# Decay rows of the first head pair: from a 66-partition sum in place instead of through DRAM, with the first constants, copies and loads reordered

## The chip, the cores and the metric

The kernel runs on one core of one Trainium2 chip. The metric is device microseconds of one launch. The profiler records one execution; its times are in microseconds from the first instruction. Engines are named as in the profile: PE multiplies matrices (PEld loads its weights), DVE, ACT and POOL work element by element, SP issues most transfers.

## What is computed

Three layers in a row. The first, causal attention with a decay from cumulative sums, is the one that the change touches:

```python
B, H, S, D = 4, 8, 576, 64
scores = (1 / np.sqrt(D)) * np.matmul(q, k.transpose(0, 1, 3, 2))
cum = np.cumsum(np.log(np.clip(f, 0.0001, 1.0)), axis=-1)        # f: (B, H, S)
decay = cum[:, :, :, None] - cum[:, :, None, :]
scores = np.where(causal, -1e9, scores + decay)                  # causal: above the diagonal
attn = np.exp(scores - scores.max(-1, keepdims=True))
attn = attn / (attn.sum(-1, keepdims=True) + 1e-9)
x = np.matmul(attn, v)                                           # 2304 tokens of 512
```

Then each token goes through the one of 8 experts that its logits choose (512 to 1024 to 512, ReLU, gated), and through a dense layer 512 to 2048 to 512 with a rational activation. The softmax takes away whatever is constant along a row, so only the term -cum of the key position has to be added to the scores.

## The kernel before, in words

**Pairs.** The 32 heads are worked off as 16 pairs of heads (`pair(p)`), four pairs to a batch element. A pair has its q and k transposed (two 64-row copies each, `rq` and `rk`, loaded at L374) and its v (L382, L383). A head's scores come in 128-row steps `i`, in the order of `steps`: head 0 with i = 2 and 3 first (384 and 512 columns), then the 64-row tails of both heads (288 columns, two halves), and the rest.

**Full precision by splitting.** The score product is made of high and low parts in the fp32r type. `kh` (L411) is the high part of k, `kl` (L416) what is left of it, `qs` (L422, L425) and `q2s` (L430) the same for q. A score tile takes two products: L456 (`kh` with `qs`) and L457 (`kl` with `q2s`), for the tails L467 and L468.

**The decay as two more rows.** Of the tile `kl` (a 64-row half for each head), two rows in the other head's half carry the sum cum/SCALE, split in a high and a low part; `q2s` holds ones there. So the second product adds the decay. `qs`, `q2s` and `kl` have two buffers each, for even and odd pairs, zeroed once by POOL at the start (L232 to L243).

**How the sums are made.** All 32 heads at once on 32 partitions, width 576: load f (L303), clip (L322), logarithm on ACT (L311), running sum (L315), high part on ACT (L329), low part on DVE (L333). Both parts are stored to DRAM as `cum_d` (L338). Every pair, the first included, then loads its four rows from there into `kl` (`load_c`, L388).

**What sets the order.** `Plan` is a list scheduler at build time. Each `plan.op` has a due time (`when`), a length in ns for each engine that may do it, needs, and buffers taken and freed. Among the operations that are ready on an engine it starts the one that is due first. The lengths and the due times (`T_STEP`, `T_TRANS`, `T_MOVE` ...) are constants in the code. Each engine and each DMA queue then does its instructions in the order that came out, so an early operation that moves can reorder all that come later in the attention stage. On PE the first 80 operations are idle matmuls on constants (`idle`, L353), before the first scores.

**Downstream of the scores.** `least` (L479, L491) takes the scores out of PSUM with the mask and the minimum, `weights` (L511, L522) makes the exponentials on ACT, PE transposes them (L598, L578), ACT or DVE copies them (`evac`, L291 and L293), and PE multiplies by v (L621). When the four pairs of a batch element are done, its five row blocks are scaled by DVE into tiles `xr` (L796, three buffers) and stored to `x_d` by POOL's queue (L823). After the last batch the token routing is computed and the expert layer starts.

Of the kernel before, what the change touches and what calls it, by code (L numbers as in the profile page):

```python
# [9 lines left out]
F32 = mybir.dt.float32  # L10
F32R = mybir.dt.float32r
# [4 lines left out]
AF = mybir.ActivationFunctionType  # L16
ALU = mybir.AluOpType
# [4 lines left out]
P = 128  # L22
# [115 lines left out]
def tile_attention_moe_mlp(  # L138
# [72 lines left out]
    oh = ec.tile([P, NE, NCOL], BF16, name="oh")  # L211
    pref = ec.tile([P, NE], F32, name="pref")
    nc.gpsimd.iota(pref, pattern=[[-1, NE]], base=NE, channel_multiplier=0, allow_small_or_imprecise_dtypes=True)

    prefs = ec.tile([P, NI, NE], F32, name="prefs")
    nc.gpsimd.tensor_copy(prefs, pref.unsqueeze(1).to_broadcast([P, NI, NE]))
    nc.gpsimd.memset(prefs[TL:, NQ], 0.0)


    with ExitStack() as actx, ExitStack() as rctx:  # L220
# [7 lines left out]


        qs = [wk.tile([P, 2, S + P], F32R, name=f"qs{i}", bufs=1) for i in range(2)]  # L230
        for t in qs:
            nc.gpsimd.memset(t.bitcast(F32)[:, :, S:], 0.0)  # L232
        half = (slice(0, D), slice(D, P))

# [3 lines left out]
        kls = [ld.tile([P, 2, S], F32R, name=f"kl{i}", bufs=1) for i in range(2)]  # L238
        for t, k in zip(q2s, kls):
            nc.gpsimd.memset(t.bitcast(F32), 0.0)  # L240
            nc.gpsimd.memset(k.bitcast(F32), 0.0)
            for h in range(2):
                nc.gpsimd.memset(t.bitcast(F32)[half[1 - h].start : half[1 - h].start + 2, h, 0:S], 1.0)  # L243

# [3 lines left out]

        mask = wk.tile([P, NQ * P], F32, name="mask", bufs=1)
        mask_t = wk.tile([P, S // 2], F32, name="mask_t", bufs=1)  # L250
        nc.gpsimd.memset(mask, 0.0)
        nc.gpsimd.memset(mask_t, 0.0)
        for t in [mask[:, (NQ - 1) * P :]] + [mask_t[h * TL : (h + 1) * TL, S // 2 - TL :] for h in range(2)]:
            nc.gpsimd.affine_select(
                out=t, in_=t, compare_op=ALU.is_ge, fill=BIG / SCALE, base=0, pattern=[[-1, t.shape[-1]]], channel_multiplier=1
            )

# [22 lines left out]
        def wt(tag, shape=(P, S)):  # L280
            return wk.tile(list(shape), F32, tag=tag, name=tag, bufs=plan.buffers.get(tag, 2))
# [17 lines left out]
        g0 = {}  # L299

        def f_load(e):
            g0["fl"] = wt("t")[:NBH]
            nc.sync.dma_start(out=g0["fl"], in_=f)  # L303

        def f_zero(e):
            g0["zf"] = wt("pr")[:NBH]
            nc.vector.memset(g0["zf"], 0.0)

        def f_log(e):
            g0["lf"] = wt("pr")[:NBH]  # L310
            nc.scalar.activation(g0["lf"], g0["fl"], AF.Ln)  # L311

        def f_scan(e):
            g0["cum"] = wt("t")[:NBH]
            nc.vector.tensor_tensor_scan(  # L315
                out=g0["cum"], data0=g0["lf"], data1=g0["zf"], initial=0.0, op0=ALU.add, op1=ALU.add
            )
# [3 lines left out]
        o_f = plan.op(early, {"SP": 1900}, f_load, takes=["t"])  # L321
        o_c = plan.op(early, {"DVE": 369}, lambda e: nc.vector.tensor_scalar(  # L322
            g0["fl"], g0["fl"], 1.0e-4, 1.0, op0=ALU.max, op1=ALU.min), [o_f])
        o_l = plan.op(early, {"ACT": 573}, f_log, [o_c], takes=["pr"], frees=[("t", o_f)])
        o_cum = plan.op(early, {"DVE": 669}, f_scan, [o_l, o_z], takes=["t"], frees=[("pr", o_z), ("pr", o_l)])

        def f_high(e):
            g0["ch"] = wt("pr")[:NBH].bitcast(F32R)
            nc.scalar.activation(g0["ch"], g0["cum"], AF.Copy, scale=1.0 / SCALE)  # L329

        def f_low(e):
            g0["cl"] = wt("pr")[:NBH].bitcast(F32R)
# [28 lines left out]
        def pair(p):  # L361
# [29 lines left out]
            for h0, h1 in one:  # L391
# [15 lines left out]
            def kh(h):  # L407
                def go(e):
                    if h == 0:
                        d["kh"] = lt("kh", (P, 2, S), F32R)  # L410
                    nc.vector.tensor_copy(d["kh"][:, h], d["rk"][:, h])  # L411
                return go
# [16 lines left out]
            def q2h(h):  # L429
                return lambda e: (nc.vector if e == "DVE" else nc.gpsimd).tensor_scalar(  # L430
                    q2[half[h], h, 0:S], d["rq"][half[h], h], 1.0, 1.0, op0=ALU.mult, op1=ALU.mult
                )
# [108 lines left out]
            for si, step in enumerate(steps):  # L541
# [4 lines left out]
                if i < NQ:  # L546
                    n, m = (i + 1) * P, len(hs)
                    need = [x[h] for h in hs for x in (o_kh, o_kl, o_qh, o_ql, o_q2)] + [l_c, pt_first[0]]
                    o_s = plan.op(w, {"PE": 2 * m * (max(n, 256) / 2.4 + 14)}, scores(hs, i, u), need, takes=["s"] if pt_first[0] else ["s", "pT"])
                    pt_first[0] = pt_first[0] or o_s  # L550
                    o_l_ = plan.op(w + T_LEAST * SPAN, {"DVE": m * (120 + 1.042 * n)}, least(hs, i, u), [o_s], takes=["t"], frees=[("s", o_s)])
                    d["o_exp"].append(None)
                    o_e = first_e = plan.op(w + T_EXP * SPAN, {"ACT": m * (360 + 0.85 * n)}, weights(hs, i, u), [o_l_], takes=["pr"], frees=[("t", o_l_)])
                    d["o_exp"][-1] = o_e
                    all_s.append(o_s)
                else:
                    prev, first_e = None, None
                    for c in (0, hw):
                        o_s = plan.op(w, {"PE": 4 * (hw / 2.4 + 14)}, scores_tail(c, u), o_kh + o_kl + o_qh + o_ql + o_q2 + [l_c, pt_first[0]], takes=["s"])
# [326 lines left out]
        plan.op(SPAN, {"SP": 1300}, load_wl, [st[0]["o_ot"]])  # L886

        with tc.manual_schedule():
            plan.emit()
# [761 lines left out]
```

## Time and profile before

| | us |
|---|---|
| median of 3 runs | 891.31 (890.9 to 892.05) |
| the profiled execution's own time | 889.93 |
| its span, first to last instruction | 888.2 |
| PE busy over the span | 849.3 (96%) |
| DVE busy | 747.9 (84%) |
| ACT busy | 615.6 (69%) |
| POOL busy | 337.5 (38%) |

The attention stage takes the first 204 us or so; the routing, the expert layer and the dense layer follow. PE's busy time counts overlapping matmuls as one stretch and hides how well a stretch is filled, so the stage is read from gaps on PE and from who ended them. The chain of work that ended last, which the page also gives, reaches back only into the expert layer, and says nothing of the first stage.

### The profile page before, as it was taken

Reading aid. Unit: us, or ns where it says so; the run is one execution under the profiler, and the core shown is the slowest. Engines: PE = TensorE matmul, PEld = TensorE weight load, DVE = VectorE, ACT = ScalarE, POOL = GpSimd, SP = SyncE. Lnnn points to the kernel's source line nnn. Section 1 sums busy time; section 2 is a strip of 40 time slices with the busy share of each in tenths; the row PEclk is TensorE's granted clock in tenths of the full one; section 3 lists DMA queues with packets and bytes.
Section 4 is the critical chain, followed back from the end, with each engine's and each line's share of the span. In section 5 each row is a group of like instructions: output and inputs, shape, how many; then the busy total and the mean of one; then the engine's idle time right before and its main releaser. Section 6 shows DMA issues by size and latency. Waiting matters only on the chain. (4 is left out here: it accounts for less than half of the span.)

```text
span 888.2 us, 15292 instructions
## 1 busy us (share of the span) xinstructions
PE 849.3 (96%) x4667; PEld 705.0 (79%) x4667; DVE 747.9 (84%) x1428; ACT 615.6 (69%) x1282; POOL 337.5 (38%) x364
## 2 busy tenths in 40 slices
PE   6999898996999999999999999999999999999997
PEld 6787786764888887888787788899888889988885
DVE  7798999778798878778876999898898878988882
ACT  4889897876465667567545878777676667777772
POOL 7888586502113232223241233343233224324222
PEclk9999999997999999999999999999999999999999
DMA  6776567604866588789564121010000001000001
GB/s 167 167 182 168 154 175 212 199 27 151 298 218 217 177 263 310 226 288 316 195 218 154 48 72 37 0 60 24 13 36 25 12 1 57 16 1 36 1 0 48
DMA packets 49130, 110.32 MB, mean 124 GB/s; under 512 B 8405, under 2 KB 12526, under 8 KB 49038
## 3 DMA queue, kind: packets, MB, share of 16 engines
q1 hardware_dynamic: 36910, 69.90, 26.4%
q0 software_dynamic: 12128, 39.34, 13.3%
q8 instruction: 40, 0.66, 0.3%
q14 instruction: 52, 0.43, 0.2%
HBM read 151.79 MB, written 20.35 MB: 194 GB/s over the span
## 5 line engine op out<-in xcount | busy, mean ns | idle before, releaser
L1519 POOL TENSOR_TENSOR gl<-raw,gh 128x512 fp32r<-128x512 f32 (+1 forms) x71 | 84.2, 1186 | 207.3 <-ACT gh L1517 127.2
L1535 PE MATMUL pa<-wu,gl 128*128 128x512 f32 x256 | 100.6, 393 | 1.1 <-POOL gl L1519 1.1
L1533 PE MATMUL pa<-wu,gh 128*128 128x512 f32 x256 | 101.2, 395 | 0.0
L1534 PE MATMUL pa<-wu,gh 128*128 128x512 f32 x256 | 100.1, 391 | 0.0
L1492 ACT ACTIVATE raw<-ph 128x512 f32<-128x512 f32 (+1 forms) x80 | 44.3, 554 | 78.1 <-PE ph L1484 74.8
L1058 DVE TENSOR_TENSOR wu<-raw,wu 128x1024 fp32r<-128x1024 f32 x64 | 75.2, 1219 | 8.0 <-ACT wu L1056 6.6
L511 ACT ACTIVATE pr<-t,mn 128x384 f32<-128x384 f32 (+3 forms) x128 | 70.7, 557 | 16.0 <-DVE mn L479 15.4
L1505 DVE SCALAR_TENSOR_TENSOR raw<-raw,coef,raw 128x512 f32<-128x512 f32 (+1 forms) x80 | 66.2, 827 | 17.8 <-ACT raw L1501 15.1
L1495 DVE SCALAR_TENSOR_TENSOR raw<-raw,babs 128x512 f32<-128x512 f32 (+1 forms) x80 | 58.3, 729 | 20.9 <-ACT raw L1493 20.2
L1482 PE MATMUL ph<-colAh,wi 128*128 128x512 f32 x192 | 74.9, 390 | 1.0 <-ACTq L1423 0.7
L1484 PE MATMUL ph<-colAh,wi 128*128 128x512 f32 x192 | 74.7, 389 | 0.0
L1483 PE MATMUL ph<-colAl,wi 128*128 128x512 f32 x192 | 74.7, 389 | 0.0
L1056 ACT ACTIVATE wu<-raw 128x1024 fp32r<-128x1024 f32 x64 | 63.8, 1066 | 4.1 <-DMA raw<-in_w_dram 2.2
L479 DVE CUSTOM_DVE_ANT_0 t<-s,mask 128x384 f32<-128x384 f32 (+3 forms) x128 | 57.8, 484 | 6.5 <-PE s L457 3.0
L1506 DVE SCALAR_TENSOR_TENSOR raw<-raw,cbias 128x512 f32<-128x512 f32 (+1 forms) x80 | 57.6, 720 | 2.3
L1500 ACT ACTIVATE raw<-raw,cbias 128x512 f32<-128x512 f32 (+1 forms) x80 | 55.0, 687 | 6.3 <-DVE raw L1495 5.8
L1494 ACT ACTIVATE raw<-ph,neg 128x512 f32<-128x512 f32 (+1 forms) x80 | 59.3, 741 | 0.0
L1535 PEld LDWEIGHTS pa<-wu,gl 128*128 128x128 f32 x256 | 48.0, 188 | 12.7 <-POOL gl L1519 2.4
L1497 DVE SCALAR_TENSOR_TENSOR raw<-raw,coef,ph 128x512 f32<-128x512 f32 (+1 forms) x80 | 55.5, 694 | 2.5
L1533 PEld LDWEIGHTS pa<-wu,gh 128*128 128x128 f32 x256 | 48.1, 188 | 9.5 <-ACT gh L1517 0.7
L1534 PEld LDWEIGHTS pa<-wu,gh 128*128 128x128 f32 x256 | 48.1, 188 | 9.0
L1507 DVE SCALAR_TENSOR_TENSOR raw<-raw,raw 128x512 f32<-128x512 f32 (+1 forms) x80 | 52.4, 655 | 2.4
(263 smaller groups left out, 2391.9 us busy)
## 6 DMA issues: line engine op xcount, KB each, us to landing
raw<-in_w_dram SPq DMA_DIRECT2D x92, 1024.0 KB
rk<-in_kT_dram SPq DMA_DIRECT2D x30, 288.0 KB
rq<-in_qT_dram SPq DMA_DIRECT2D x30, 288.0 KB
d<-in_w_in_dram POOLq DMA_DIRECT2D x16, 512.0 KB
d<-in_w_out_dram POOLq DMA_DIRECT2D x16, 512.0 KB
y_d<-ys SPq DMA_DIRECT2D x22, 256.0 KB
v<-in_v_dram SPq DMA_DIRECT2D x16, 256.0 KB
wo_d<-d POOLq DMA_DIRECT2D x16, 256.0 KB
```

The costliest lines, as they stand in the source:

```text
L511: nc.scalar.activation(u["pr"][:, sl], u["t"][:, sl], AF.Exp, bias=u["mn"][:, m : m + 1], scale=-1.0, accum_out=sm[:, i, 2 * hp + h : 2 * ...
L1056: nc.scalar.activation(w[:, 0], r, AF.Copy)
L1058: nc.vector.tensor_tensor(w[:, 1], r, w[:, 0].bitcast(F32), ALU.subtract)
L1482: nc.tensor.matmul(out_, wh, hi[:, :, c], start=(c == 0), stop=False)
L1483: nc.tensor.matmul(out_, wh, lo[:, :, c], start=False, stop=False)
L1484: nc.tensor.matmul(out_, wl_, hi[:, :, c], start=False, stop=(c == KD - 1))
L1494: nc.scalar.activation(u_, ph, AF.Identity, scale=neg[:, 3:4], bias=neg[:, 2:3])
L1505: nc.vector.scalar_tensor_tensor(u_, u_, coef[:, 0:1], rr, ALU.subtract, ALU.mult)
L1519: low.tensor_tensor(d["gl"], d["u_"], d["gh"].bitcast(F32), ALU.subtract)
L1533: nc.tensor.matmul(a_, gh[:, sl], wh, start=(m == 0), stop=False)
L1534: nc.tensor.matmul(a_, gh[:, sl], wl_, start=False, stop=False)
L1535: nc.tensor.matmul(a_, gl[:, sl], wh, start=False, stop=(m == MF - 1))
```

## The change

- **Sums.** The sum is made over 66 partitions: rows 32 to 63 hold the 32 heads as before, rows 64 and 65 both hold head 0, and rows 0 to 31 all hold head 1 (of which rows 0 and 1 are used). So head 0's rows end up on the partitions where pair 0's `kl` wants them, and so do head 1's. A per-partition factor `sgn` gives on partitions 0 and 64 the high part, on 1 and 65 the low part. `f_rows` writes these pairs of rows straight into `kl` of pair 0, one two-row DVE instruction per head. Pair 0 has no `load_c`.
- **Loads of f.** Three instead of one: two on SP's queue, one on ACT's, ahead of the table load.
- **Stores of the sums.** Still made, for pairs 1 to 15, but due later, and the low part (`f_low`) is due later too; `f_rows(1)` and `f_low` also need a `least` of pair 0 each.
- **First constants.** `kl` of pair 0 is zeroed by DVE, `after` and `onesb` come first on POOL, then what pair 0 needs, then the mask and the identity, then pair 1's buffers, the small tables last.
- **Copies.** For pair 0, `q2s` of both heads and `kh` of head 1 go from DVE to ACT.
- **Coefficients.** The two loads of `coef` move from the start into the plan, after pair 1.

```diff
+    sgn = ec.tile([P, 2], F32, name="sgn")
+    nc.vector.memset(sgn, 1.0 / SCALE)
+    for r in (0, D):
+        nc.vector.memset(sgn[r : r + 1, 0:1], -1.0 / SCALE)
+        nc.vector.memset(sgn[r : r + 1, 1:2], 0.0)
...
+        def blank(i, on):
+            t = q2s[i].bitcast(F32)
+            on.memset(kls[i].bitcast(F32), 0.0)
+            nc.gpsimd.memset(t, 0.0)
...
+        blank(0, nc.vector)
...
         def f_load(e):
-            g0["fl"] = wt("t")[:NBH]
-            nc.sync.dma_start(out=g0["fl"], in_=f)
+            g0["fl"] = wt("t")
+            nc.scalar.dma_start(out=g0["fl"][D:NF], in_=f[0:1, :].to_broadcast([2, S]))
+            nc.sync.dma_start(out=g0["fl"][F0], in_=f)
+            nc.sync.dma_start(out=g0["fl"][0:NBH], in_=f[1:2, :].to_broadcast([NBH, S]))
+            nc.scalar.preload_act_table_set("natural_log_exp_and_others")
...
+        def low_of(rows, to):
+            nc.vector.scalar_tensor_tensor(
+                to, g0["cum"][rows], sgn[rows, 1:2], g0["ch"][rows].bitcast(F32), ALU.mult, ALU.subtract
+            )
+
+        def f_rows(h):
+            r = half[1 - h].start
+            return lambda e: low_of(slice(r, r + 2), kls[0][r : r + 2, h, :])
...
-        o_cl = plan.op(early, {"DVE": 669}, f_low, [o_ch], takes=["pr"], frees=[("t", o_cum)])
+        o_first = [plan.op(early, {"DVE": 669}, f_rows(0), [o_ch], takes=["c"])]
+        o_first.append(plan.op(-1.2 * SPAN, {"DVE": 669}, f_rows(1), [o_ch]))
+        o_cl = plan.op(-1.1 * SPAN, {"DVE": 669}, f_low, [o_ch], takes=["pr"], frees=[("t", o_cum)])
         o_cst = [
-            plan.op(early, {"SP": 650}, f_store(0, "ch"), [o_ch], frees=[("pr", o_ch)]),
-            plan.op(early, {"SP": 650}, f_store(1, "cl"), [o_cl], frees=[("pr", o_cl)]),
+            plan.op(-0.9 * SPAN, {"SP": 650}, f_store(0, "ch"), [o_ch], frees=[("pr", o_ch)]),
+            plan.op(-0.9 * SPAN, {"SP": 650}, f_store(1, "cl"), [o_cl], frees=[("pr", o_cl)]),
         ]
...
-            l_c = plan.op(tl + 0.3 * SPAN, {"SP": 1200}, load_c, o_cst, takes=["c"])
+            l_c = plan.op(tl + 0.3 * SPAN, {"SP": 1200}, load_c, o_cst, takes=["c"]) if p else o_first[0]
...
-                o_kh.append(plan.op(w, {"DVE": 420}, kh(h), [lk[h]] + o_kh[:1], takes=["kh"] if h == 0 else []))
+                o_kh.append(plan.op(w, {"DVE": 420} if p or h == 0 else {"ACT": 620}, kh(h), [lk[h]] + o_kh[:1], takes=["kh"] if h == 0 else []))
...
-                q2e = {"POOL": 1340} if p else {"DVE": 400}
+                q2e = {"POOL": 1340} if p else {"ACT": 620}
...
+                    if p == 0 and si < 2:
+                        (o_first[1], o_cl)[si].needs.append(o_l_)
...
+        plan.op(2 * SPAN, {"SP": 1300}, load_coef, [st[1]["o_ot"]])
```

**Order on SP, at the start.** From the loads of head 1's k of pair 0 (64x576) on; the loads of 64x1152 are those of pair 1. Before:

```order
L374 DMA rk<-in_kT_dram 64x576 x2
L338 DMA cum_d<-pr 32x576
L374 DMA rq<-in_qT_dram 64x576 x2
L902 DMA coef<-in_ca_dram 128x4
L903 DMA coef<-in_cb_dram 128x2
L338 DMA cum_d<-pr 32x576
L382 DMA v_129<-in_v_dram 128x2x256
L383 DMA v_129<-in_vt_dram 64x2x64
L388 DMA kl_119<-cum_d 2x576 x2
L374 DMA rk<-in_kT_dram 64x1152 x2
L374 DMA rq<-in_qT_dram 64x1152 x2
L388 DMA kl_120<-cum_d 2x576 x2
```

Now:

```order
L407 DMA rk<-in_kT_dram 64x576 x2
L407 DMA rq<-in_qT_dram 64x576 x2
L415 DMA v_142<-in_v_dram 128x2x256
L416 DMA v_142<-in_vt_dram 64x2x64
L407 DMA rk<-in_kT_dram 64x1152 x2
L407 DMA rq<-in_qT_dram 64x1152 x2
L369 DMA cum_d<-pr 32x576 x2
L415 DMA v_143<-in_v_dram 128x2x256
L416 DMA v_143<-in_vt_dram 64x2x64
L421 DMA kl_113<-cum_d 2x576 x2
L407 DMA rk<-in_kT_dram 64x1152 x2
L407 DMA rq<-in_qT_dram 64x1152 x2
```

Pair 1's loads of k and q stand ahead of the stores of the sums; the stores, v of pair 1, the decay rows of pair 1 (`kl_113`) and then k of pair 2 follow them.

**Order on DVE, at the start, now.** L356 is `low_of`, L517 a `least` (before: L479), L331 to L339 clip and running sum, L459 the low part of q:

```order
L327 MEMSET pr 66x576
L331 TENSOR_SCALAR t<-t 66x576
L339 SCALAR_TENSOR_TENSOR t<-pr 66x576
L306 CAST kh<-rk 128x576
L450 TENSOR_TENSOR kl_112<-rk,kh 64x576
L356 SCALAR_TENSOR_TENSOR kl_112<-t,sgn,pr 2x576
L459 TENSOR_TENSOR qs_108<-rq,qs_108 64x576
L450 TENSOR_TENSOR kl_112<-rk,kh 64x576
L517 ISA t,mn<-s,mask 128x384
```

After it come the two rows of head 1, L459 of head 1, the 512-wide `least`, and only then the low part of the 32 heads (L356 with 32x576). Before, that low part (L333) stood right behind `kl` of head 0, and both L430 and the copy `kh` of head 1 were on DVE ahead of the first `least`.

**Order on DVE, where the rows of the second batch element are scaled.** `xr` numbers tell tiles apart, `t` rows are `least`. Before, from the second of the five on (the first stands 25 rows earlier):

```order
L796 TENSOR_TENSOR xr_2547<-pt_2533,rg_1526 128x512
L491 ISA t_2556,mn_2557<-s_2539,mask_135 128x288
L491 ISA mn_2557 128x1
L796 TENSOR_TENSOR xr_2570<-pt_2559,rg_1526 128x512
L491 ISA t_2556,mn_2557<-s_2565,mask_t_136,mn_2557 128x288
L491 ISA mn_2557 128x1
L293 COPY pT_2590<-pt_2574 128x3x128
L796 TENSOR_TENSOR xr_2598<-pt_2583,rg_1526 128x512
```

Now, from the first of the five on:

```order
L836 TENSOR_TENSOR xr_2600<-pt_2589,rg_1483 128x512
L836 TENSOR_TENSOR xr_2613<-pt_2595,rg_1483 128x512
L529 ISA t_2623,mn_2624<-s_2608,mask_119 128x288
L529 ISA mn_2624 128x1
L836 TENSOR_TENSOR xr_2631<-pt_2617,rg_1483 128x512
L529 ISA t_2623,mn_2624<-s_2626,mask_t_120,mn_2624 128x288
L529 ISA mn_2624 128x1
L836 TENSOR_TENSOR xr_2650<-pt_2639,rg_1483 128x512
```

The first scaled block has moved next to the second, so four of the five follow each other at once, with three buffers between them.

## Rows read from the trace of the kernel before

**Rows 1.** The page, busy times: us, share of the span, instructions.
```profile
PE 849.3 (96%) x4667; PEld 705.0 (79%) x4667; DVE 747.9 (84%) x1428; ACT 615.6 (69%) x1282; POOL 337.5 (38%) x364
```

**Rows 2.** Windows: each line a stretch, its length, busy us, PEclk, DMA share, GB/s.
```profile
core 0: us, PE busy (x) PEld busy (x) DVE busy (x) ACT busy (x) POOL busy (x), PEclk, DMA share, GB/s
8.78:13.57 4.79, 0.45 (x5) 0.21 (x3) 3.88 (x5) 0.89 (x2) 4.55 (x12) 1.00 0.34 99
13.57:25.13 11.56, 8.74 (x46) 7.53 (x47) 8.40 (x27) 7.86 (x24) 7.76 (x20) 0.81 1.00 231
34.00:194.00 160.00, 151.02 (x1244) 122.02 (x1242) 142.42 (x481) 133.82 (x425) 107.17 (x106) 1.00 0.60 163
204.00:208.00 4.00, 0.00 (x0) 0.00 (x0) 3.90 (x10) 4.00 (x16) 0.00 (x0) 0.62 0.63 217
```

**Rows 3.** Timeline of pair 0: start, length, engine, line, what [idle before <-releaser].
```profile
0.82 0.41 SPq L303 DMA_DIRECT2D t<-in_f_dram  x1
2.75 0.45 DVE L322 TENSOR_SCALAR t<-t 32x576 f32<-32x576 f32 x1 [1.22 <-DMA t<-in_f_dram]
...
5.22 0.50 DVE L411 CAST kh<-rk 128x576 fp32r<-128x576 f32 x1
...
6.41 0.68 ACT L422 ACTIVATE qs<-rq 128x576 fp32r<-128x576 f32 x1 [0.40 <-DMA rq<-in_qT_dram]
6.51 0.74 DVE L333 SCALAR_TENSOR_TENSOR pr<-t,pr 32x576 fp32r<-32x576 f32 x1
...
8.73 0.36 SPq L338 DMA_DIRECT2D cum_d<-pr  x1
...
12.06 0.58 SPq L388 DMA_DIRECT2D kl<-cum_d  x2
...
13.57 0.41 PE L457 MATMUL s<-kl,q2s 128*128 128x384 f32 x1 [4.35 <-DMA kl<-cum_d]
...
14.14 0.56 DVE L479 CUSTOM_DVE_ANT_0 t<-s,mask 128x384 f32<-128x384 f32 x1 [1.42 <-POOL s L921]
...
14.87 0.69 DVE L479 CUSTOM_DVE_ANT_0 t<-s,mask 128x512 f32<-128x512 f32 x1 [0.17 <-PE s L457]
```

**Rows 4.** Timeline, from the loads of pair 1 to its first scores.
```profile
12.69 1.13 SPq L374 DMA_DIRECT2D rk<-in_kT_dram  x2
13.87 1.24 SPq L374 DMA_DIRECT2D rq<-in_qT_dram  x2
...
18.38 1.42 POOL L416 TENSOR_TENSOR kl<-rk,kh 64x576 fp32r<-64x576 f32 x1 [2.64 <-DVE kh L411]
18.65 1.47 DVE L411 CAST kh<-rk 128x576 fp32r<-128x576 f32 x1
...
21.37 1.25 ACT L422 ACTIVATE qs<-rq 128x576 fp32r<-128x576 f32 x2 [1.08 <-DMA rq<-in_qT_dram]
22.13 1.41 POOL L425 TENSOR_TENSOR qs<-rq,qs 64x576 fp32r<-64x576 f32 x1 [0.47 <-ACT qs L422]
23.62 0.67 POOL L430 TENSOR_SCALAR q2s<-rq 64x576 fp32r<-64x576 f32 x1
...
25.13 0.67 PE L456 MATMUL s<-kh,qs 128*128 128x384 f32 x1
```

**Rows 5.** Windows, two stretches in which the granted clock was low.
```profile
13.90:17.20 3.30, 3.30 (x14) 3.09 (x13) 2.24 (x8) 2.12 (x6) 1.76 (x14) 0.50 0.99 246
24.10:27.20 3.10, 2.83 (x11) 2.33 (x10) 1.33 (x4) 1.92 (x8) 2.24 (x3) 0.50 1.07 237
```

**Rows 6.** Timeline, the scaled rows of the second batch element and a store.
```profile
147.14 0.69 DVE L796 TENSOR_TENSOR xr<-pt,rg 128x512 f32<-128x512 f32 x1
...
157.30 0.63 DVE L796 TENSOR_TENSOR xr<-pt,rg 128x512 f32<-128x512 f32 x1
...
158.22 0.59 POOL L823 DMA_DIRECT2D x_d<-xr  x1 [3.13 <-DVE xr L796]
...
164.58 0.68 DVE L796 TENSOR_TENSOR xr<-pt,rg 64x512 f32<-64x512 f32 x1 [2.91 <-DMA x_d<-xr]
```

More of the change, by code (lines that the diff above doesn't have):

```diff
@@ L227, in tile_attention_moe_mlp, with edge @@
         ps_o = actx.enter_context(tc.tile_pool(name="ps_o", bufs=2, space=PSUM))
+        half = (slice(0, D), slice(D, P))
         qs = [wk.tile([P, 2, S + P], F32R, name=f"qs{i}", bufs=1) for i in range(2)]
-        for t in qs:
-            nc.gpsimd.memset(t.bitcast(F32)[:, :, S:], 0.0)
-        half = (slice(0, D), slice(D, P))
         q2s = [wk.tile([P, 2, S + P], F32R, name=f"q2s{i}", bufs=1) for i in range(2)]
         kls = [ld.tile([P, 2, S], F32R, name=f"kl{i}", bufs=1) for i in range(2)]
-        for t, k in zip(q2s, kls):
-            nc.gpsimd.memset(t.bitcast(F32), 0.0)
-            nc.gpsimd.memset(k.bitcast(F32), 0.0)
+        def blank(i, on):
+            t = q2s[i].bitcast(F32)
+            on.memset(kls[i].bitcast(F32), 0.0)
+            nc.gpsimd.memset(t, 0.0)
             for h in range(2):
-                nc.gpsimd.memset(t.bitcast(F32)[half[1 - h].start : half[1 - h].start + 2, h, 0:S], 1.0)
+                nc.gpsimd.memset(t[half[1 - h].start : half[1 - h].start + 2, h, 0:S], 1.0)
+            nc.gpsimd.memset(qs[i].bitcast(F32)[:, :, S:], 0.0)
+        blank(0, nc.vector)
+        mask = wk.tile([P, NQ * P], F32, name="mask", bufs=1)
+        mask_t = wk.tile([P, S // 2], F32, name="mask_t", bufs=1)
+        def edge(t):
+            nc.gpsimd.affine_select(
+                out=t, in_=t, compare_op=ALU.is_ge, fill=BIG / SCALE, base=0, pattern=[[-1, t.shape[-1]]], channel_multiplier=1
+            )
+        nc.gpsimd.memset(mask, 0.0)
+        edge(mask[:, (NQ - 1) * P :])
+        identf = const.tile([P, P], F32, name="identf")
+        make_identity(nc, identf)
+        nc.gpsimd.memset(mask_t, 0.0)
+        for h in range(2):
+            edge(mask_t[h * TL : (h + 1) * TL, S // 2 - TL :])
+        blank(1, nc.gpsimd)
         vs = [ld.tile([P, 2, NI, D], F32, name=f"v{i}", bufs=1) for i in range(3)]
@@ L247, in tile_attention_moe_mlp @@
             nc.gpsimd.memset(t[: P - TL, :, NQ], 0.0)
[L249 to L256, printed above, removed]
+        pref = ec.tile([P, NE], F32, name="pref")
+        nc.gpsimd.iota(pref, pattern=[[-1, NE]], base=NE, channel_multiplier=0, allow_small_or_imprecise_dtypes=True)
+        prefs = ec.tile([P, NI, NE], F32, name="prefs")
+        nc.gpsimd.tensor_copy(prefs, pref.unsqueeze(1).to_broadcast([P, NI, NE]))
+        nc.gpsimd.memset(prefs[TL:, NQ], 0.0)
         CUT = NQ // 2
@@ L321, in tile_attention_moe_mlp @@
         o_f = plan.op(early, {"SP": 1900}, f_load, takes=["t"])
-        o_c = plan.op(early, {"DVE": 369}, lambda e: nc.vector.tensor_scalar(
-            g0["fl"], g0["fl"], 1.0e-4, 1.0, op0=ALU.max, op1=ALU.min), [o_f])
+        o_c = plan.op(early, {"DVE": 369}, f_clip, [o_f])
         o_l = plan.op(early, {"ACT": 573}, f_log, [o_c], takes=["pr"], frees=[("t", o_f)])
@@ L429, in q2h, with go @@
             def q2h(h):
-                return lambda e: (nc.vector if e == "DVE" else nc.gpsimd).tensor_scalar(
-                    q2[half[h], h, 0:S], d["rq"][half[h], h], 1.0, 1.0, op0=ALU.mult, op1=ALU.mult
-                )
+                def go(e):
+                    to, x = q2[half[h], h, 0:S], d["rq"][half[h], h]
+                    if e == "ACT":
+                        nc.scalar.activation(to, x, AF.Copy)
+                    else:
+                        nc.gpsimd.tensor_scalar(to, x, 1.0, 1.0, op0=ALU.mult, op1=ALU.mult)
+                return go
             for h in range(2):
                 w = ts + h * T_SPLIT2 * SPAN
-                o_kh.append(plan.op(w, {"DVE": 420}, kh(h), [lk[h]] + o_kh[:1], takes=["kh"] if h == 0 else []))
+                o_kh.append(plan.op(w, {"DVE": 420} if p or h == 0 else {"ACT": 620}, kh(h), [lk[h]] + o_kh[:1], takes=["kh"] if h == 0 else []))
                 o_qh.append(plan.op(w + 1, {"ACT": 720}, qh(h), [lq[h]] + o_qh[:1], takes=["q"] if h == 0 else []))
@@ L547, in pair @@
                     n, m = (i + 1) * P, len(hs)
-                    need = [x[h] for h in hs for x in (o_kh, o_kl, o_qh, o_ql, o_q2)] + [l_c, pt_first[0]]
+                    need = [x[h] for h in hs for x in (o_kh, o_kl, o_qh, o_ql, o_q2, l_cs)] + [pt_first[0]]
                     o_s = plan.op(w, {"PE": 2 * m * (max(n, 256) / 2.4 + 14)}, scores(hs, i, u), need, takes=["s"] if pt_first[0] else ["s", "pT"])
@@ L558, in pair @@
                     for c in (0, hw):
[L559 removed]
+                        o_s = plan.op(w, {"PE": 4 * (hw / 2.4 + 14)}, scores_tail(c, u), o_kh + o_kl + o_qh + o_ql + o_q2 + l_cs + [pt_first[0]], takes=["s"])
                         prev = plan.op(w, {"DVE": 130 + 1.042 * hw}, least_tail(c, u), [o_s, prev], takes=[] if c else ["t"],
@@ L886, in tile_attention_moe_mlp, with load_coef @@
         plan.op(SPAN, {"SP": 1300}, load_wl, [st[0]["o_ot"]])
+        coef = const.tile([P, 6], F32, name="coef")
+        def load_coef(e):
+            nc.sync.dma_start(out=coef[:, 0:4], in_=ca.to_broadcast([P, 4]))
+            nc.sync.dma_start(out=coef[:, 4:6], in_=cb.to_broadcast([P, 2]))
+        plan.op(2 * SPAN, {"SP": 1300}, load_coef, [st[1]["o_ot"]])
         with tc.manual_schedule():
```

45 lines of the change are left out of this document (20 added, 25 removed).

## The prediction

> **What bounds the kernel now.** I read the page first: PE is busy for 96% of the span, every other engine clearly less [rows 1]. That is an average, so I went to the stage that the change touches, by windows [rows 2]. The reader should see three things there. Between 8.78 and 13.57 PE is busy for 0.45 of 4.79 us. From 13.57 to 25.13 it has 8.74 of 11.56, with a granted clock of 0.81 on the mean. From 34 to 194, over the later pairs, it is busy for 151.02 of 160, with all engines well filled: there the stage runs on PE's and DVE's own work, not on loads. At 204 to 208 PE has nothing: the routing waits for the whole attention stage, so what the stage ends sooner, the rest starts sooner. I found nothing behind it that is tied to a time of its own, and carry a shift of the stage to the end one to one.
>
> Then the timeline of the start [rows 3]. PE's first second product (L457) starts at 13.57 after 4.35 idle, and what releases it is the load of `kl` from `cum_d`: the low part is made at 6.51, its store issued at 8.73, the load at 12.06. So pair 0 pays a trip through DRAM of 13.57 - 8.73 = 4.84 us. The timeline of pair 1 [rows 4] shows the next limit: its first scores stand at 25.13, behind POOL's `ql` and `q2s` (until 23.62 + 0.67 = 24.29), these behind ACT's `qs` at 21.37, and that behind the load of q, whose issue ended at 13.87 + 1.24 = 15.11. It landed 21.37 - 15.11 = 6.26 us after that, in a stretch in which the transfers moved 231 GB/s [rows 2].
>
> **The change, part by part.**
>
> *First scores of pair 0.* The second load of f on SP costs one more issue, 0.41, so the clip can start at 3.16 instead of 2.75. DVE's memset ended at 2.75 - 1.22 = 1.53 [rows 3]; the memset of `kl` (1152 columns, at most twice the 0.74 of the 576 columns of L333) and the tiny ones bring that to 3.3 at most. I shift the chain by 0.5. The two-row instruction has the same 576 columns, so I price it as L333, and it takes L333's place: 7.0 to 7.75. The low part of q follows until 8.5; ACT's `qs` at 6.41 + 0.5 and a copy of 0.68 for `q2s` are done by 8.3. The second product can start at 8.7 instead of 13.57. The third load of f is on ACT's queue beside these and costs nothing unless it lands last; then its price is another 0.4 in the same chain.
>
> *From there to pair 1.* Now DVE is the limit of pair 0. Ahead of the low part of the 32 heads stand `kl` and `ql` of head 1, its two rows, and two `least`: 3 x 0.74 + 0.56 + 0.69 = 3.5, then the low part itself 0.74: 8.5 + 4.2 = 12.7, with 0.3 for the waits between, 13.0. The stores go at 13.0, the load of pair 1's rows 12.06 - 8.73 = 3.33 later, and its data another 1.51 (12.06 to 13.57) later: 17.9. K and q of pair 1 are no longer behind that. SP's issues ahead of them are two of f and five pairs of k, q and v, at 1.24 a pair: 0.82 + 0.82 + 6.2 = 7.8, so with k and q themselves (2.4) q is out at 10.2 instead of 15.11, and with the same 6.26 on hand at 16.5 instead of 21.37. DVE's copy `kh` of pair 1 follows three more `least` (0.56 each): 13.0 + 1.7 + 0.5 = 15.2. POOL's `kl` 1.42, `q2s` 0.67 and `ql` 1.41 give 18.7, and PE follows 0.84 later as before (24.29 to 25.13): 19.6. **So pair 1 starts 5.5 us sooner.** The bounds: 17.9 + 0.3 if POOL were not last, 6.9 sooner; 3.5 sooner if each link above is half a microsecond late.
>
> *What is late next.* K of pair 2 is behind the stores and behind pair 1's rows on SP: 16.3 + 0.6 for these, 2.4 for its own k and q, so q is out at 19.3, landed at 25.6 by the same 6.26, through half of ACT's 1.25 and POOL's 1.41 at 27.7. At 10 us per pair (160 us for sixteen) pair 2 is wanted at 19.6 + 10 = 29.6, and 0.84 less for PE's own lead. The margin is 1 us, so I let the 5.5 pass.
>
> *Clock.* PE's clock was at its lower level, 1.2 GHz (0.50), from 13.9 to 17.2 and from 24.1 to 27.2 [rows 5], both times after PE had idled. That costs half of 3.3 and of 3.1. The first lies in time that is now DVE's; before pair 1 a gap on PE remains, so I expect the second one to stay. I take 0; the other end is 1.6 gained.
>
> *Row stores.* DVE's fifth scaled block of the second batch element waited 2.91 for the buffer of the second, written until 157.30 + 0.63 = 157.93, stored by POOL from 158.22 and free at 164.58: 6.65 after it was written [rows 6]. The first block, at 147.14, was ten microseconds ahead and cost no wait. Now four blocks follow each other, and the fourth needs the first one's buffer. Between them lie two blocks (0.69 each) and two `least` of at most 0.56, 2.5 us; 6.65 - 2.5 = 4.15 of waiting in place of 2.91: **1.2 lost.** ACT and PE stand behind DVE there. Bounds: nothing, if the store lands sooner, and 4.2, if the first batch element, whose blocks move together too, adds another 3.
>
> *The rest.* Memsets on POOL change places but are nearly all the same; they stay ahead of POOL's first work for pair 1 at 15.2. `kh` of head 1 and the two `q2s` go from DVE to ACT, which has 0.89 busy of 4.79 there [rows 2]. The coefficients are loaded before anything wants them. The later order is dealt anew by the planner, with the same instructions; PE's idle time in it is 160 - 151.02 = 9.0 us, and I take a third of that, 3 us either way, as noise, and 0 as the value.
>
> **Sum:** -5.5 + 0 + 1.2 = -4.3. The profiled execution took 889.93, so 885.6 against it; it lies 1.4 below the median of the runs, 891.31, against which I give the forecast: **887.0 us**.
>
> **A rule that speaks against it.** The copy `kh` (L411) took 0.50 at 5.22 [rows 3], but 1.47 at 18.65, where POOL's `kl` ran from 18.38 to 19.80 [rows 4]: 0.97 more beside POOL. The clip and `kh` of head 0 run while POOL writes its constants, in which it hardly pauses (4.55 of 4.79 us busy in the stretch behind them [rows 2]), and half a microsecond later than before they meet other instructions of it; two such delays make 1.9.
> The Trainium skill (SBUF — State Buffer, "Who interferes with whom") says that GpSimd and VectorE in its two-port modes share one pair of ports, which an instruction holds as an exclusive lock until it is done. The long copy at 18.65 agrees with it; by that rule the first chain would be later by such waits, and the sum smaller, not of another sign.
>
> **The rivals.**
> - *DVE blocked by POOL at the start.* The mechanism above, two waits of 0.97: the start gains 3.6, the sum is -2.4, the time 888.9. For it: POOL has no pause there. Against: the clip took 0.45 at 2.75 and the copy 0.50 at 5.22, both undisturbed.
> - *The trip through DRAM moves to pair 1* (slower). Pair 1's rows are made from 13.0 on, before from 6.51. If the store and the load each take the 6.26 that loads took in the busy stretch, they land at 13.0 + 6.26 + 0.6 + 6.26 = 26.1, and PE starts pair 1 at 26.4, 1.3 later than before; with the 1.2 of the row stores 893.8. The point from which it decides: a landing after 24.8 takes the whole start gain. For it: SP issues v of pair 1 right ahead. Against: q of pair 1 has landed at 16.5, and while SP waits for the stores little is in flight. Half of it ends within the noise, near 890.5.
> - *The ring of three row buffers* (slower). If in both batch elements the fourth and fifth block wait, at most 6.65 each time, DVE waits 13.3 in place of 2.91: +10.4 against -5.5, 896.2. Waits at that line of over 8.4 in sum take all the gain. For it: the first two blocks follow each other at once. Against: in the first batch element other work lies between them.
> - *A full clock* in pair 1 and an order with less idle time: another 1.6 and 1.5, 883.9.
>
> That the rows don't go in place I rule out: in the new order no load of `kl` stands ahead of pair 0's scores.
>
> **How the numbers follow.** Forecast 0.52, blocked DVE 0.16, the trip moved 0.14, the ring 0.10, the better case 0.08. The range takes the forecast with its bounds: -6.9 - 1.6 = -8.5 at the lower end, and -3.5 + 4.2 = +0.7 at the upper: 883 to 892. The two slower cases in full, and the unlikeliest of the others, stay out, less than 0.2. About 0.2% (1.8 us) is what a measurement of this kernel can tell from no change. Faster: most of the forecast, the better case and two thirds of the blocked one, 0.67. Slower: half of the two slower rivals, 0.12. Within: 0.21.
>
> **What would show it.** Right: the first second product of pair 0 (L495, before L457) near 8.7, with no transfer as releaser; pair 1's first scores near 19.6, released by POOL or DVE; PE's busy time per 160 us in the later pairs near 151; one wait of about 4 us at the scaled rows (L836, before L796). Wrong: pair 1's first L495 released by the load of `kl` after 24; or an early start and a stage that nevertheless ends at the same time, with the gap on PE or DVE in the later pairs.

## The result and the profile after

The changed kernel is **slower**: 905.23 us median of four runs (902.22 to 907.47) against 891.68 for the kernel before on the same chip, a ratio over the runs (not that of the two medians) of 1.0144 with an interval of 1.0105 to 1.0183. The profiled execution took 904.29 with a span of 902.6. The forecast was 887.0.

The page's busy line, and windows (a stretch, its length, busy us per engine, PEclk, DMA share, GB/s):

```profile
PE 856.1 (95%) x4667; PEld 709.7 (79%) x4667; DVE 746.8 (83%) x1424; ACT 621.8 (69%) x1294; POOL 337.1 (37%) x363
```

```profile
10.00:20.00 10.00, 6.85 (x39) 5.94 (x37) 6.62 (x21) 5.95 (x16) 9.04 (x28) 0.83 0.64 160
20.00:30.00 10.00, 8.35 (x60) 6.16 (x60) 6.21 (x24) 8.54 (x28) 7.74 (x7) 1.00 1.00 235
34.00:194.00 160.00, 143.43 (x1117) 114.84 (x1115) 129.43 (x423) 125.49 (x393) 102.29 (x103) 0.98 0.60 160
0.00:217.40 217.40, 189.53 (x1486) 152.22 (x1486) 172.04 (x570) 165.49 (x518) 133.63 (x160) 0.97 0.58 151
175.00:181.00 6.00, 4.39 (x16) 3.79 (x17) 5.11 (x16) 3.57 (x11) 2.32 (x6) 0.50 0.25 75
```

The third line answers to the third of [rows 2]: in the same 160 us PE is busy for 143.43 instead of 151.02, and DVE for 129.43 instead of 142.42. The fourth covers the attention stage with its 1486 matmuls and ends 4.1 us before the routing's first matmul; in the kernel before, the stretch that does so ends at 204.5:

```profile
0.00:204.50 204.50, 182.47 (x1486) 148.07 (x1486) 173.48 (x573) 159.70 (x506) 133.82 (x161) 0.98 0.60 161
```

The routing's first matmul, before and after, from the timelines of PE:

```profile
208.64 0.31 PE L1026 MATMUL pid<-rs,op__3306 128*128 128x25 f16 x5 [5.69 <-DVE op__3306 L1021]
221.50 0.31 PE L1069 MATMUL pid<-rs,op__3314 128*128 128x25 f16 x5 [4.87 <-DVE op__3314 L1064]
```

So nearly all of the loss is in this stage: 12.9 us of the 14.4 between the two profiled spans (888.2 and 902.6). Of these PE idles 27.87 - 22.03 = 5.8 more, and is busy 7.1 more for the same matmuls.

The timeline of the start, answering to [rows 3, 4]:

```profile
3.54 0.46 DVE L331 TENSOR_SCALAR t<-t 66x576 f32<-66x576 f32 x1 [0.54 <-DMA t<-in_f_dram]
7.26 0.81 DVE L356 SCALAR_TENSOR_TENSOR kl<-t,sgn,pr 2x576 fp32r<-2x576 f32 x1
9.07 0.33 PE L495 MATMUL s<-kl,q2s 128*128 128x384 f32 x1
...
10.74 2.55 SPq L369 DMA_DIRECT2D cum_d<-pr  x2
12.16 0.81 DVE L356 SCALAR_TENSOR_TENSOR pr<-t,sgn,pr 32x576 fp32r<-32x576 f32 x1
...
17.08 0.68 ACT L456 ACTIVATE qs<-rq 128x576 fp32r<-128x576 f32 x1 [1.30 <-DMA rq<-in_qT_dram]
18.22 1.41 POOL L459 TENSOR_TENSOR qs<-rq,qs 64x576 fp32r<-64x576 f32 x1
18.45 0.56 SPq L421 DMA_DIRECT2D kl<-cum_d  x2
19.75 0.42 PE L494 MATMUL s<-kh,qs 128*128 128x384 f32 x1
```

The first second product stands at 9.07 (13.57 before), pair 1's first scores at 19.75 (25.13 before). The start came out as forecast, and the time was lost behind it. A mark that every pair has shows where: its tail transposes (L582 before, L622 after), start in us, read from the timelines of PE:

| pair | 0 | 1 | 2 | 3 | 4 | 5 | 6 | 7 | 8 | 9 | 10 | 11 | 12 | 13 | 14 | 15 |
|---|---|---|---|---|---|---|---|---|---|---|---|---|---|---|---|---|
| before | 20.3 | 34.6 | 45.0 | 55.0 | 64.4 | 74.9 | 85.5 | 95.2 | 107.6 | 120.1 | 129.9 | 139.5 | 152.4 | 168.9 | 179.9 | 189.0 |
| after | 19.1 | 31.9 | 42.4 | 51.9 | 61.5 | 76.1 | 88.8 | 97.0 | 106.2 | 125.4 | 134.8 | 144.3 | 156.1 | 183.0 | 191.1 | 198.9 |
| two due times (below) | 19.0 | 31.0 | 40.4 | 49.7 | 59.1 | 71.6 | 79.9 | 89.8 | 102.2 | 116.3 | 127.6 | 137.3 | 151.7 | 165.8 | 178.9 | 187.9 |

The changed kernel leads by 2.9 at pair 4; it loses at pairs 5 and 6, at pair 9, and 10 us at pair 13. (A mark's place among the other work moves with the order, so a single step of the table is only a hint.) At pair 13, answering to [rows 6], the timeline of all engines:

```profile
166.33 0.60 SPq L908 DMA_DIRECT2D raw<-in_w_dram  x1
166.81 1.22 DVE L836 TENSOR_TENSOR xr<-pt,rg 128x512 f32<-128x512 f32 x2
167.74 1.17 POOL L863 DMA_DIRECT2D x_d<-xr  x2 [1.17 <-DVE xr L836]
168.33 0.69 DVE L836 TENSOR_TENSOR xr<-pt,rg 128x512 f32<-128x512 f32 x1
...
175.86 0.69 DVE L836 TENSOR_TENSOR xr<-pt,rg 128x512 f32<-128x512 f32 x1 [6.42 <-DMA x_d<-xr]
176.61 1.06 PE L830 MATMUL pt<-identf,ot 128*64 128x128 f32 x4 [5.67 <-DVE xr L836]
...
176.99 0.51 ACT L549 ACTIVATE pr<-t,mn 128x256 f32<-128x256 f32 x1 [6.30 <-DVE mn L517]
```

Three scaled blocks fill the ring; the fourth waits 6.42 for the first one's store, PE and ACT behind it. After that pause PE's clock is granted at 0.50, 1.2 GHz (the window 175 to 181 above), where I estimate that half of PE's 4.39 busy us, 2.2, is the price of the clock. Before, PE is busy for all of 171 to 181 at the full clock:

```profile
171.00:181.00 10.00, 10.00 (x91) 7.75 (x91) 7.02 (x29) 8.35 (x28) 3.38 (x5) 1.00 0.11 43
```

### The profile page after: what moved, and what is told of

Its sections match the earlier page's. It is cut to its first block, busy times and chain, and to the rows that moved or that the text cites. A ratio compares the mean times of both kernels' runs of the same rounds, so it can differ in the third digit from the quotient of the medians.

```text
span 902.6 us, 15300 instructions
## 1 busy us (share of the span) xinstructions
PE 856.1 (95%) x4667; PEld 709.7 (79%) x4667; DVE 746.8 (83%) x1424; ACT 621.8 (69%) x1294; POOL 337.1 (37%) x363
## 5 line engine op out<-in xcount | busy, mean ns | idle before, releaser
L1525 PE MATMUL ph<-colAh,wi 128*128 128x512 f32 x192 | 74.9, 390 | 1.6 <-DVE raw L1540 0.8
L517 DVE CUSTOM_DVE_ANT_0 t<-s,mask 128x384 f32<-128x384 f32 (+3 forms) x128 | 58.4, 485 | 10.9 <-PE s L495 5.4
L638 PE MATMUL pt<-identf,pr 128*128 128x128 f32 x320 | 49.6, 279 | 5.2 <-ACT pr L549 3.8
```

Of the source, the lines that this page charges most:

```text
L1525: nc.tensor.matmul(out_, wh, hi[:, :, c], start=(c == 0), stop=False)
```

## The experiments

**Whose loss is it: the order's, or the new work's?** Theory 1: the order dealt anew to the later pairs. Theory 2: the new loads, constants and copies. Theory 3: the ring alone. In three runs a table of operations (an engine's letter and the operation's number) stands in for the planner. A deal sets more than the order: for many operations the planner also chooses between DVE and ACT. Of these, 59 stand on the other of the two in the later order of before (tables of *a_old_later* and, below, *a_load_late*), so "order" here means order and engine together, and no run tells the two apart.

```diff
-        for o in self.order():
-            o.emit(o.engine)
+        for word in SEQ.split():
+            self.ops[int(word[1:])].emit(ENGINE_OF[word[0]])
```

*a_old_later*, the changed kernel with the later order of before. 

> The changed kernel with its start as it is, and every operation from the second pair's splitting on in the order of the kernel before, written out as a table in place of the planner's. Theory 1 (the start gains as forecast, and the loss is the order that the planner deals to the later pairs): the lead of 2.7 us that the tail transposes of pair 2 show is kept to the end, so 887 to 889 us, and the fourth and fifth scaled rows of the second batch element wait about 3 us again instead of 6.42. Theory 2 (the loss comes from the new loads, constants and copies themselves, whatever the order): within 2 us of the changed kernel, 903 to 907. Theory 3 (only the ring of three row buffers): as theory 1 if the waits go, since the order sets them.

Measured: 891.0, ratio 0.9981 (0.9960 to 1.0002). The wait at the scaled rows is 3.1, at the fifth block as before, and the loss is gone, but so is the lead: the tails stand at 32.3 in pair 1 and at 44.8 in pair 2, so it went at my seam between the two orders, and the 887 to 889 expected for theory 1 was missed.

*a_old_all*. 

> The changed kernel with the order of before throughout, the start too: the new row pieces go just ahead of the work that reads them, the low part and the stores of the running sum stand where they stood before. Theory 1: the first pair's scores begin a little later than in the changed kernel, but the later pairs run as before, so 886 to 891 us. Theory 2: 903 to 907.

Measured: 889.39, ratio 0.9974 (0.9951 to 0.9997), as theory 1 expected. With the old order throughout, the new loads, constants and copies cost nothing.

*b_new_later*, the mirror. 

> The kernel before, with its old start through DRAM, and every operation from the second pair's splitting on in the order of the changed kernel. Theory 1: the loss comes over without the change: 891.7 plus what the changed kernel lost after its lead of 2.7, 13.5 + 2.7 = 16, so 903 to 910 us. Theory 2: within 2 us of 891.7.

Measured: 908.46, ratio 1.0166 (1.0131 to 1.0201). The order alone carries the loss into a kernel without the change, and with it the wait at the fourth block, 6.2 there. Theory 2 falls.

**The ring.** In `wt`, the number of buffers alone (cut from its line):

```diff
-bufs=plan.buffers.get(tag, 2))
+bufs={"xr": 5}.get(tag) or plan.buffers.get(tag, 2))
```

> The changed kernel in its own order, with five buffers instead of three for the scaled rows. Theory 1: the order has other waits than this, so it gains about the 6.42 us of the wait at the fourth block less what is taken up behind it, 898 to 902 us. Theory 3 (the ring alone makes the loss): 887 to 892. If other work covers the wait: 904 to 906.

> The kernel before in its own order, with five buffers for the scaled rows. Theory 1: its wait of 2.91 us goes, and at most that reaches the end: 889 to 892. If the ring by itself is what costs, the gain is as large as in the changed kernel, 7.5: 884.

Measured: the changed kernel 897.7, ratio 1.0058 (1.0037 to 1.0079), so 0.0086 or 7.7 us better; the kernel before 889.48, 0.9981 (0.9961 to 1.0000), 1.7 better, at the edge of its interval. The 7.7 is a little more than the wait of 6.42, which fits a pause that also costs clock. In the timelines of PE the step from pair 12's tails to pair 13's is 16.5 us before, 26.9 in the changed kernel and 20.2 with five buffers. Theory 3 as the whole cause falls, since the changed kernel stays slower.

**What made the store land so late.** One issue on SP is moved in the order table (1162 is the weight load, 1069 the load of the last pair's rows):

```diff
-S1162
 S1069
+S1162
```

> The changed kernel in its own order but for one issue on SP: the fourth 1024 KB load of expert weights (L908), issued at 166.33 just ahead of the row stores of the second batch element (first at 167.74), goes behind the load of the last pair's decay rows, which SP issued at 179.83; PE, DVE, ACT and POOL have the same instructions in the same order. If the row store lands so late because it shares the transfers with that load: the wait of 6.42 at the fourth scaled block falls to 0 to 3 us, PE does not stand still for 5.67 and keeps its clock, and the time falls by 3.5 to 7.5 us (what the five buffers gave), 898 to 902. If the three buffers and POOL's own stores set the wait, whatever else is in flight: 903 to 907.

Measured: 899.53, ratio 1.0089 (1.0051 to 1.0128), 0.0055 or 4.9 us better than the changed kernel by the ratios; the two intervals overlap, and one of the seven executions took 907.3, so the trace has to decide. Its timeline of the same place:

```profile
168.38 1.17 POOL L863 DMA_DIRECT2D x_d<-xr  x2 [1.17 <-DVE xr L836]
...
172.65 0.69 DVE L836 TENSOR_TENSOR xr<-pt,rg 128x512 f32<-128x512 f32 x1 [2.57 <-DMA x_d<-xr]
...
173.40 0.63 PE L830 MATMUL pt<-identf,ot 128*64 128x128 f32 x4 [1.82 <-DVE xr L836]
...
175.83 0.40 SPq L908 DMA_DIRECT2D raw<-in_w_dram  x1
```

and windows, the changed kernel first, this run second:

```profile
166.00:180.00 14.00, 7.95 (x47) 6.90 (x47) 7.51 (x22) 5.01 (x16) 3.68 (x9) 0.82 0.56 173
```

```profile
166.00:180.00 14.00, 10.97 (x83) 9.72 (x82) 10.69 (x34) 8.66 (x25) 6.54 (x11) 1.00 0.46 155
```

From the store's issue to the free buffer it is 172.65 - 168.38 = 4.27 instead of 175.86 - 167.74 = 8.12, and PE keeps its full clock. With nothing else changed in any engine's order, the late landing is shown to come from the 1024 KB load beside it. The Trainium skill (DMA: Bandwidth & Descriptors, "Queues, rings and completion order") says that each DMA engine takes turns between the queues that have work for it, a packet at a time; the later landing fits that, but no run here shows the turns themselves.

The load is not new, however. In the kernel before it stood 2.1 us ahead of the store that DVE waits for in [rows 6]:

```profile
156.14 0.58 SPq L868 DMA_DIRECT2D raw<-in_w_dram  x1
```

From that store's issue to the free buffer it took 164.58 - 158.22 = 6.36. In the traces of *a_old_all*, *b_new_later* and the run with two due times below it took 7.5 to 7.9, with the load 0.1 to 1.4 us ahead. So of these traces only that of *a_load_late* lacks the late landing, and only in the new order does it stop PE for long: in *a_old_all* the store takes 163.11 - 155.45 = 7.66 and DVE waits 4.14, but at the fifth block, and PE waits for that line 0.9 in all, against 6.8 in the changed kernel.

**Due times.** `T_STEP` and its neighbours say when a step is wanted. Two were chosen among many so that the planner, by its own lengths, ends early; no operation is added or taken away, only order and engine differ (DVE has 1441 instructions instead of 1424, ACT 1277 instead of 1294):

```diff
-        T_STEP = (0.003, 0.167, 0.576, 1.046, 0.372, 0.855, 1.261)
+        T_STEP = (0.003, 0.167, 0.576, 1.046, 0.347, 0.855, 1.261)
...
-        T_LEAST, T_EXP, T_SPLIT, T_SPLIT2 = 0.096, 0.218, 0.342, 0.209
+        T_LEAST, T_EXP, T_SPLIT, T_SPLIT2 = 0.096, 0.218, 0.318, 0.209
```

> The changed kernel with two due times set anew (the fifth of T_STEP from 0.372 to 0.347 of a pair's span, T_SPLIT from 0.342 to 0.318), among those with which the planner, by its own lengths, ends earliest; nothing that runs is added or taken away, only the order differs. Theory 1 (the loss is the order dealt with due times that were set for the old start): the loss of 16 after the lead goes, 885 to 890 us, and the tail transposes of pairs 5, 6, 9 and 13 come about as early as in the kernel before or 2 us earlier. Theory 2 (the loss lies in the new start's loads, constants and copies): 903 to 907.

> As the run with the two due times, and five buffers for the scaled rows. Theory 1: what the ring costs depends on the order; if the fourth block of the second batch element waits 3 us as in the kernel before, the wait goes and 0 to 3 us of it reach the end: 883 to 888 us. Theory 3 (the ring alone): the same as the five buffers alone gave, 897.7, less nothing.

Measured: 888.68, ratio 0.9972 (0.9958 to 0.9986), and with five buffers 888.42, 0.9977 (0.9960 to 0.9994). Both beat the kernel before and the changed one; the table above has the first one's tails. It leads by 5.3 at pairs 3 and 4. Of that, 1.0 is left at pair 15 (188.95 - 187.92). With five buffers the profiled execution, at 886.63 the fastest of its twelve, still leads by 4.5 there; the median gains nothing clear from the buffers, although a wait of 3.75 at the fifth block goes.

The opposite test: the kernel *before*, with one due time nudged by about 0.05 us.

```diff
-        T_BATCH, T_BATCHJ, T_ROWS = 0.299, 0.239, -5.772
+        T_BATCH, T_BATCHJ, T_ROWS = 0.299, 0.244, -5.772
```

> The kernel before with one due time nudged, T_BATCHJ from 0.239 to 0.244 of a pair's span, about 0.05 us; the start, the loads and every instruction are the old ones, and the order is the same up to pair 8's scores. Theory 1: an order dealt anew with due times that fit the old one only loses, since the old one was the best of its neighbours: 3 to 12 us slower, 895 to 904. If a new deal is noise about zero, as the prediction took it: 889 to 895.

> The kernel before with the same due time nudged the other way, T_BATCHJ from 0.239 to 0.234 of a pair's span. If a new deal with due times that fit the old order only loses: slower in this direction too, 893 to 899, less than the 6 of the other nudge or as much. If it is noise about zero, the two nudges should differ in sign: 884 to 890.

Measured: up 897.66, ratio 1.0074 (1.0055 to 1.0093); down 897.6, 1.0070 (1.0046 to 1.0095). Slower on both sides, by some 6 us. Among these three the old order is the good one; for both nudges a new deal only lost.

**What the start gains.** Each half of the change was undone in the kernel with two due times. *a_due_trip* replaces the pieces made in place, and moves the low part and the stores ahead of them:

```diff
-            return lambda e: low_of(slice(r, r + 2), kls[0][r : r + 2, h, :])
+            return lambda e: nc.sync.dma_start(out=kls[0][r : r + 2, h, :].bitcast(F32), in_=cum_d[h])
```

> As the run with the two due times, but the first pair's decay rows take the old trip: the low part, both stores and the reload from DRAM come first, in the old places of SP's queue, and the pieces made in place are gone; constants, copies and all other order stay. If the rows made in place are what gives the start its lead (5.3 us at the tail transposes of pairs 3 and 4): the first second product falls back from 9 to 13 to 14 us, the second pair's first scores from 19.6 to about 24, and the end from 888.7 to 891 to 894. If the order of constants and copies gives the lead: 888 to 890.

*a_due_const* puts the constants back into their old order, among them:

```diff
-        blank(0, nc.vector)
+        for t, k in zip(q2s, kls):
+            nc.gpsimd.memset(t.bitcast(F32), 0.0)
+            nc.gpsimd.memset(k.bitcast(F32), 0.0)
```

> As the run with the two due times, but POOL's constants are made in the old order (identity and preference first, all blanks before the masks, the first pair's blank of the low-part rows on POOL again); rows in place and all planned order stay. If the rows alone give the lead, this costs nothing: 888 to 890. If they only work because the blanks come first on POOL and DVE, the first pieces wait for POOL, whose constants took till about 15 us in the kernel before: the first second product falls back by 2 to 5 us, and the end to 890 to 894.

Measured: 892.8, ratio 0.9994 (0.9970 to 1.0019), and 890.76, 0.9987 (0.9972 to 1.0003). These intervals overlap that of 0.9972, so the end does not tell the halves apart, and I go by the tails at pair 4 of one execution each: 62.2 and 61.0 against 59.1, a lead of 3.1 for the rows in place and 1.9 for the constants. With the trip, the second product waits for the load again:

```profile
12.87 0.66 PE L495 MATMUL s<-kl,q2s 128*128 128x384 f32 x1 [3.56 <-DMA kl<-cum_d]
```

With the old constants, DVE and POOL in this run:

```profile
2.88 1.28 POOL L244 MEMSET q2s<- 128x1408 f32 x1
4.09 1.06 POOL L245 MEMSET kl<- 128x1152 f32 x1
7.76 1.05 POOL L245 MEMSET kl<- 128x1152 f32 x1
8.87 1.39 POOL L247 MEMSET q2s<- 2x576 f32 x2
```

```profile
3.40 2.07 DVE L322 TENSOR_SCALAR t<-t 66x576 f32<-66x576 f32 x1 [1.70 <-DMA t<-in_f_dram]
7.49 1.64 DVE L297 CAST kh<-rk 128x576 fp32r<-128x576 f32 x1
9.23 0.75 DVE L441 TENSOR_TENSOR kl<-rk,kh 64x576 fp32r<-64x576 f32 x1
10.01 0.81 DVE L347 SCALAR_TENSOR_TENSOR kl<-t,sgn,pr 2x576 fp32r<-2x576 f32 x1
```

The rows come at 10.01 instead of 7.26, 2.75 later. The clip takes 2.07 beside POOL's memsets instead of the 0.46 above, and the copy `kh`, begun at 7.49, 1.64 instead of the 0.43 that it has in the changed kernel: 1.61 + 1.21 = 2.8 us, which is all of it.

**The rest of the loss.** With five buffers some 9 us remain between the new order (897.7) and the one with two due times. I suspected changes of matmul tile form (the rows and columns of the array that a matmul uses, 128*128 or 128*64 in the rows). In the changed kernel ten of sixteen pairs have their two products of probabilities and v apart on PE. The timelines of PE, after first, the run with two due times second:

```profile
23.88 2.28 PE L661 MATMUL po<-pT,v 128*64 128x320 f32 x20
...
31.05 0.87 PE L661 MATMUL po<-pT,v 128*64 128x256 f32 x8
```

```profile
27.66 2.93 PE L661 MATMUL po<-pT,v 128*64 128x320 f32 x28
```

Counted in PE's timelines to the end of attention, the form changes 48 times before and with two due times, 56 with either nudge, 72 after. Three runs with order tables, whose edits are these moves on PE, written as PE's order in short (621 is the line of `po` before, 661 after); in the two *a_join* runs what hangs on the moved product moves with it on DVE and ACT too:

```diff
-[L621 x20] [L621 x8] [next piece]
+[L621 x20] [next piece] [L621 x8]
```

> The kernel before with one edit in its order on PE alone: in 15 of the 16 pairs the second of the two products of probabilities and v (8 matmuls of tile form 128*64) goes one step later, behind the next piece of PE's work, so that some 28 more changes of tile form stand in PE's order; DVE, ACT, POOL and SP have the same order. If a change of form costs PE about what stands as idle of its weight loads at them in the changed kernel (0.17 to 0.20 us each): 28 x 0.18 = 5, 894 to 898 us. If it is hidden: 890 to 893.

```diff
-[L661 x20] ... [L661 x8]
+... [L661 x20] [L661 x8]
```

> The changed kernel with the two products of probabilities and v of a pair together on PE again in the ten pairs in which they stood apart (the first one is put off to the second), what hangs on it following; the rest of its order is kept. If the changes of form and the waits that hang on the products apart make the rest of the loss: 20 changes x 0.2 = 4 us at least and 8 at most less than the changed kernel, 897 to 901 us. If the rest lies in the order of the scores, rows and copies: 903 to 907.

> As the run with the products together, and five buffers for the scaled rows. If the row stores (7.5 us with the five buffers) and the products apart (4 to 8) are two separate causes: 905.2 - 7.5 - 4 to 8 = 890 to 894 us. If they are one and the same wait: no less than the five buffers alone, 896 to 899.

Measured: b_split 893.62, ratio 1.0026 (1.0005 to 1.0047), with 72 changes, as many as the changed kernel: 2.3 us for 24 more, 0.1 each, half of what I had put. The Trainium skill (TensorEngine Tiling (Array Packing), "Key Properties") says that a change of tiling mode drains the engine; the run fits that in that the changes aren't free, but no trace here shows a drain by itself. a_join went the wrong way: 915.26, 1.0270 (1.0236 to 1.0304), although it has 55 changes. Putting off the first product made others late: waits of PE's transposes for ACT's exponentials, of the waits by line to the end of the stage,

```profile
PE pt L638 <- ACT pr L549: 9.5, 12, 1.7
```

against 3.8 in the changed kernel, whose longest are these:

```profile
PE pt L830 <- DVE xr L836: 6.8, 2, 5.7
PE s L494 <- DVE mn L517: 5.3, 4, 1.8
PE pt L638 <- ACT pr L549: 3.8, 6, 1.2
```

Columns: total us, times, longest. These 5.7 more are part of the 10 us that it lost; the rest is not accounted for. With five buffers it is 908.24, 1.0185 (1.0155 to 1.0215): again 7.6 better, so the ring is a cause of its own. By b_split the candidate explains 2 to 3 us. The other 6 or so no run here gives to one instruction, nor says whether order or engine makes them: that stays open.

## Why the prediction was wrong

- **First scores of pair 0**: right. Forecast 8.7 with no transfer as releaser, measured 9.07, and a clip at 3.54 (forecast 3.25).
- **Pair 1's first scores**: right, 19.75 for 19.6, with the low part at 12.16 for 13.0, and POOL ahead of them as forecast. The load of its rows was issued at 18.45, two late, and still in time. One sub-step was not: I had given the constants' order nothing, and it carries 1.9 of the lead.
- **What is late next**: right where the order allows it. With two due times all 5.3 reach pairs 3 and 4.
- **Carrying a shift to the end one to one**: it held behind the stage (12.9 us later at the routing, 14.4 at the end), and failed inside it. Of 5.3 in the run with two due times 1.0 is left at the last pair's tails; in the medians 2.8 us (888.68 against 891.45 in its comparison) arrive.
- **Clock**: the first low stretch of [rows 5] stayed, only earlier (11.3 to 14.6 at 0.53), the second did not (20 to 30 at 1.00); a new one came at 175 to 181, behind the ring's wait.
- **Row stores**: right mechanism, wrong size. The sum had a wait of 4.15, a loss of 1.2, from a hold of 6.65 after the write [rows 6]. The wait was 6.42: the store freed its buffer 8.12 after its issue, where [rows 6] have 6.36. I had taken that for the store's own time, but a 1024 KB weight load stood ahead of it in both; without one it takes 4.27. With PE's stop and its clock the ring was worth 7.7 in the new order against 1.7 in the old: a term of about 6, not 1.2. The rival was to take all the gain from 8.4 us of waits at that line; one wait of 6.42 cost about as much, since I had priced DVE's wait alone and not the clock behind it.
- **The rest**: **this step failed.** "The later order is dealt anew by the planner ... 3 us either way, as noise, and 0 as the value." With the same operations, in part on other engines, two due times make 905.23 or 888.68, 16.5 us in the medians; the new order in the old kernel costs 1.66%; and either nudge in the old one costs 0.7%. The term was not small, and all three deals with due times that had not been set for them (the changed kernel's and the two nudges') lost; that the old due times were tuned to the old order is what this suggests, not more. A third of PE's idle time was the wrong measure: a bad order adds idle time and makes the busy time longer too, 7.1 of 12.9. The forecast's own sign of being wrong, an early start with the gap in the later pairs, is what came. Which waits make the part that is not the ring's, some 9 us, stays open.
- **The rivals**: DVE's wait for POOL did not occur (clip 0.46), but it does with the old constants, 2.8 us for the 1.9 of the forecast: the change escapes it because it also moves the constants. The trip did not move to pair 1: a landing after 24.8 was its point, and PE started at 19.75. No rival of mine was a worse order by itself; the nearest, the ring, at 896.2 and 0.10, had a third of the loss.

## What to carry to other kernels

Where a planner with tuned constants sets the order, a change at its input is two changes: the one written, and a new order; measure the second by nudging one of its constants, and tune again before judging the first. In any order, look for what the queues issue just ahead of a store that a ring of buffers waits for, and don't take a store's time from a place with a load beside it for the store's own. Here a wait that stopped PE for 5.67 was followed by a stretch at half clock, so the wait alone was too low a price.

## What had not been expected

A row store freed its buffer 4.27 us after its issue with no 1024 KB load beside it, and 6.36 to 8.12 with one issued 0.1 to 2.1 us ahead, in five traces. A stop of PE of 5.67 us was followed by a stretch at 0.50 up to 181, and two extra buffers gave back 7.7 us for a wait of 6.42. And a due time moved by 0.05 us, with every operation the same, cost 6 us in either direction.
